# Attention probabilities turned as two halves of 64 queries, in PSUM places of two banks, with a new issue order

## The chip, the core and the metric

The kernel runs on one core of a Trainium2 chip. A core has five engines with queues of their own, which work in order and wait for each other by semaphores: TensorE (PE, matmuls, with weight loads shown apart as PEld), VectorE (DVE), ScalarE (ACT), GpSimd (POOL) and SyncE (SP, which issues DMAs). TensorE's results go to PSUM, eight banks of 512 float32 columns on each of 128 partitions; ScalarE and VectorE read them from there. The metric is the time of the device for one execution, in microseconds (us).

## The reference

Two stages follow each other. The first is attention over 8 batches, 8 heads, 576 positions and 64 channels, with a mask by blocks of 64 positions; the second sends each of the 4608 tokens to one of 8 experts, and at most `capacity` (80) tokens per expert are computed.

```python
scores = scale * np.matmul(q, k.transpose(0, 1, 3, 2))
mask = block_i >= block_j                       # blocks of 64 positions
scores = np.where(mask, scores, -1000000000.0)
scores = scores - np.max(scores, axis=-1, keepdims=True)
attn = np.exp(scores)
attn = attn / (np.sum(attn, axis=-1, keepdims=True) + 1e-09)
out = np.matmul(attn, v)                        # [batch, head, 576, 64]
...
logits = x @ w_gate                             # x: 4608 tokens x 512
expert_idx = np.argmax(logits, axis=1)          # gate_w: the softmax's value there
h = np.maximum(x[tok_idx] @ w1[e], 0.0)         # at most 80 tokens per expert, by gate_w
out[tok_idx] = gate_w[tok_idx, None] * (h @ w2[e])
```

## The kernel before

The attention stage works on 32 pairs of heads, four to a batch. A pair's 576 queries are five row tiles: 0 to 3 have 128 queries each, tile 4 has 64. Row tile u needs the keys up to 128 x (u + 1), so its scores are 128 wide for tile 0 and 512 for tile 3. What a turn does for a pair is cut into pieces (methods of `Pair`):

- `scores(g)` (L428, L435): matmuls of 64 channels each; one head uses the upper and one the lower 64 rows of the array. Group "3" is row tile 3, "20" row tiles 2 and 0, "1" row tile 1. `scores_4` (L444) is row tile 4. They write to one of two PSUM places of two banks (pool `ps_s`, name `sc`).
- `max` (L449), `max_4` (L453): VectorE's maxima, negated. `soft` (L457), `soft_4` (L462): ScalarE's exponentials from PSUM to SBUF (`P`), with the sums of the rows.
- `back(x)` (L490): TensorE turns blocks of 128 queries by 128 keys of the probabilities, so that the keys come to lie on the partitions. One call fills one PSUM bank with four blocks (pool `ps_m`, four banks, name `pm`). "30" and "31" are row tile 3 of either head, "20" the last blocks of tiles 2 and 0, "2" and "1" the others of tiles 2 and 1, "4" row tile 4, "44" its last, narrow block.
- `take("back", x)`: ScalarE (L522) or VectorE (L524) copies such a bank to SBUF (`PT`). The table `TAKE` names the engine.
- `values` (L510): TensorE multiplies the values by `PT`; `take("values", ...)` copies the result to `xT`.
- `prep` (L410, L413): the next pair's q and k are transposed in 32 x 32 blocks by VectorE, and q is scaled by POOL. `flip` (L278): VectorE transposes `xT` for the store.
- `step`: one of the side steps that follow each batch (the logits and the gate), in three places of a turn, over the three turns that begin three turns behind that of the batch's last pair: reciprocal, store and first logits in the first; second logits and two times their transposes and products in the second; gate, spreading and turning in the third.

The order is written out by hand: the list `TURN` is walked once per turn, and each entry (d, piece, ...) issues a piece of the pair d turns ahead or behind. Each engine's queue is the order in which its pieces stand there, and each piece's instructions wait for what they read and for the buffers that they write.

Of the kernel before, what the change touches and what calls it, by code (L numbers as in the profile page):

```python
# [7 lines left out]
F32 = mybir.dt.float32  # L8
# [16 lines left out]
CHUNK = 80  # L25


TAKE = {"back": {"30": "v", "31": "a", "1": "a", "2": "a", "20": "v", "4": "v", "44": "v"}, "values": {0: "a", 1: "a"}}

GROUPS = {"3": ((3, 0),), "20": ((2, 0), (0, 384)), "1": ((1, 0),)}  # L30

# [11 lines left out]
    (0, "max", "20"),
    (0, "soft", 3, 0),
    (0, "soft", 3, 1),
    (-1, "values", 0),
    (0, "soft", 0, 0),
    (0, "soft", 0, 1),
    (-1, "values", 1),
    (0, "step"),  # L50
    (1, "prep", 0),
    (0, "soft", 2, 0),
    (0, "soft", 2, 1),
    (0, "scores", "1"),
    (0, "max", "1"),
    (0, "back", "30"),
    (0, "back", "31"),
    (0, "step"),
    (0, "scores_4"),
    (1, "prep", 1),  # L60
    (-1, "take", "values", 0),
    (0, "take", "back", "31"),
    (0, "take", "back", "30"),
    (0, "soft", 1, 0),
    (0, "soft", 1, 1),
    (0, "max_4"),
    (0, "back", "20"),
    (0, "back", "2"),
    (0, "soft_4"),
    (0, "take", "back", "20"),  # L70
    (0, "take", "back", "2"),
    (-1, "take", "values", 1),
    (0, "step"),
    (0, "back", "1"),
    (0, "take", "back", "1"),
    (-2, "flip"),
)


# [1 line left out]
def tile_attn_moe(ctx, tc, q, k, v, w_gate, w1, w2, capacity, out, xs=None, dbg=None):  # L81
    nc = tc.nc
    B, H, S, D = q.shape
# [40 lines left out]
    for i in range(4):  # L124
        r = slice(32 * i, 32 * i + 32)
# [120 lines left out]
    Pt = []  # L246
    for i in range(2):
        row = [pb.tile([P, 2, P * (t + 1)], F32, name=f"P{i}_{t}") for t in range(NT - 1)]
        Pt.append(row + [pb.tile([P, P * NT], F32, name=f"P{i}_4")])

    VT = [pb.tile([P, 2, D], F32, name=f"vt{i}") for i in range(3)]

# [1 line left out]
    qk = att.enter_context(tc.tile_pool(name="qk", bufs=2, **right))  # L254
    attp = ExitStack()
    ps_s = attp.enter_context(tc.tile_pool(name="ps_s", bufs=2, space=PSUM))
    ps_m = attp.enter_context(tc.tile_pool(name="ps_m", bufs=4, space=PSUM))

    class Batch:
        def __init__(self, b):  # L260
# [27 lines left out]
        def logits(self, half):  # L288

            q0, q1 = ((0, 384), (384, 576))[half]  # L290
            if half == 0:
                self.lgT = sm.tile([P, S], F32, name="lgT", bufs=1)
            lt = ps_m.tile([P, 512], F32, name="pm")
            for pr in range(NP):
                nc.tensor.matmul(lt[32 * pr:32 * pr + 32, 0:q1 - q0], lhsT=wgd[:, pr, :],
                                 rhs=self.xT[:, pr, q0:q1], start=True, stop=True, tile_position=(0, 32 * pr))
            nc.scalar.copy(self.lgT[:, q0:q1], lt[:, 0:q1 - q0])

        def logits2(self, half, ends=(4, NT)):
            la = ps_m.tile([P, 512], F32, name="pm")  # L300
            rs = self.rs
            if half == 0:
                self.lg = sm.tile([P, NT, E], F32, name="lg", bufs=2)
            t0, t1 = (0, *ends)[half:half + 2]
            for t in range(t0, t1):
                n = tokn(t)
                self.turned = nc.tensor.transpose(la[0:n, P * (t - t0):P * (t - t0 + 1)],
                                                  self.lgT[:, tok0(t):tok0(t) + n], ident)
            for u0, u1, n in ((t0, min(t1, NT - 1), P), (NT - 1, t1, BLK)):
                if u0 < u1:  # L310
                    nu = u1 - u0
                    iv = la[0:n, P * (u0 - t0):P * (u1 - t0)].rearrange("p (r c) -> p r c", r=nu * NP)[:, :, 0:2 * E]
# [42 lines left out]

        def turn2(self):
            sp = self.sp
            tp = ps_m.tile([P, 512], F32, name="pm")
            for s_ in range(2):
                for g in range(4):  # L360
                    self.last = nc.tensor.matmul(
                        tp[32 * g:32 * g + 32, 0:8 * NT], lhsT=sameR3[:, 16 - 16 * s_:48 - 16 * s_],
                        rhs=sp[:, 2 * g + s_].rearrange("p t a -> p (t a)"), start=(s_ == 0), stop=(s_ == 1),
                        tile_position=(0, 32 * g))
            nc.vector.tensor_copy(Wt[:, :, :, self.b, :].rearrange("p h t a -> p t a h"),
                                  tp[:, 0:8 * NT].rearrange("p (t a h) -> p t a h", t=NT, h=2))
# [11 lines left out]
    class Pair:  # L378
# [87 lines left out]
        def back(self, x):  # L466


            if x == "30":
                self.PT = big.tile([P, 2, 13, P], F32, name="PT")  # L470
            PT = self.PT
            row = Pt[self.i % 2]
            pt = ps_m.tile([P, 512], F32, name="pm")
            if x in ("30", "31"):
                h = int(x[1])
                blocks = [(3, h, j) for j in range(4)]
                dst = PT[:, h, 3:13:3]
            elif x in ("1", "2"):
                u = int(x)
                blocks = [(u, h, j) for h in range(2) for j in range(2)]  # L480
                dst = PT[:, :, u:u + 4:3]
            elif x == "20":
                blocks = [b for h in range(2) for b in ((0, h, 0), (2, h, 2))]
                dst = PT[:, :, 0:9:8]
            else:
                blocks = [(4, None, j) for j in (range(4) if x == "4" else (4,))]
                dst = PT[:, :, 10:12] if x == "4" else PT[:, 0, 7]
            for n_, (u, h, j) in enumerate(blocks):
                src = row[u] if h is None else row[u][:, h]
                nc.tensor.transpose(pt[:, P * n_:P * (n_ + 1)], src[:, P * j:P * (j + 1)], ident)  # L490
            src = pt[:, 0:P * len(blocks)]
            if len(dst.shape) == 3:
                src = src.rearrange("p (j c) -> p j c", c=P)
            elif len(dst.shape) == 4:
                src = src.rearrange("p (h j c) -> p h j c", h=2, c=P)
            self.out["back", x] = (dst, src)

        def values(self, half):

            av = ps_m.tile([P, 512], F32, name="pm")  # L500
            PT = self.PT
            for j in range(4 + half):
                for h in range(2):
                    lhs = self.vt[:, h, :] if j == 4 else self.vn[:, h, j, :]
                    if half == 0:
                        rhs, c0, end = PT[:, h].rearrange("p b c -> p (b c)")[:, 512 * j:512 + 384 * j], P * j, 512
                    else:
                        b = PT[:, 0, 7] if j == 4 else PT[:, j // 2, 10 + j % 2]
# [128 lines left out]
    for h in (1, 0):  # L637
        pl = pall[h]
# [273 lines left out]
    with tc.For_i(0, again, 1):  # L912
# [24 lines left out]
        step = 1.0  # L937
# [161 lines left out]
```

## Time and profile before

| | |
|---|---|
| Median of 3 runs | 505.89 us (503.77 to 506.04) |
| The profiled execution | 505.98 us, span 504.1 us |
| Busy in the span | PE 465.5 us (92%), DVE 315.6 (63%), ACT 253.8 (50%), POOL 52.8 (10%) |
| First exponential to the last pair's | 11.35 to 350.86 us |
| End of the attention stage | 372.51 us |
| Mean granted clock of TensorE | 0.989 |

Each turn begins, as counted here, with the first exponential of row tile 3 on ScalarE (L457, 128 x 512). A row of a timeline gives the start from the beginning of the span, how long the instruction took, engine, line, operation, what it writes and reads, and how many are merged in the row; in brackets stands the idle time before it, and what ended it. An instruction's length is longer than the distance to the next one where an engine overlaps the end of one with the beginning of the next.

### The profile page before, as it was taken

To read this page: it belongs to the slowest core of one execution; us is meant where nothing else is said; L and a number is where in the kernel's file an instruction comes from. 1 tells how busy PE (TensorE), PEld (TensorE's weight loads), DVE (VectorE), ACT (ScalarE), POOL (GpSimd) and SP (SyncE) were. 2 spreads that over 40 slices of the span, in tenths; PEclk is the share of its full clock that TensorE was granted. 3 is DMA by queue.
4 is the path that set the end of the run, shared out by engine and by line. 5 is a ranking of instruction groups with operands and counts; after the bars stand their busy time and mean duration, and the time that the engine had idled before them with its cause. 6 is when DMAs were issued, how large, how long until landed. Compare 5 with 4: busy or idle time off the path is not lost. (4 is left out here: it accounts for less than half of the span.)

```text
span 504.1 us, 10559 instructions
## 1 busy us (share of the span) xinstructions
PE 465.5 (92%) x3887; PEld 263.1 (52%) x3887; DVE 315.6 (63%) x636; ACT 253.8 (50%) x795; POOL 52.8 (10%) x120
## 2 busy tenths in 40 slices
PE   6999989999999999999999999899877999999993
PEld 3666556556556656655665665565554333333330
DVE  4777787878788788868887886978583311211120
ACT  2776577667556766766665775667520110011000
POOL 1110301010010101001000100100025300100010
PEclk9999999999999999999999999999997999999998
DMA  5776467358647866776688588595484999979110
GB/s 93 135 131 113 75 110 138 61 97 157 106 80 157 178 156 129 148 175 139 147 166 182 129 161 180 117 282 130 167 238 103 349 385 372 411 276 387 56 43 15
DMA packets 232937, 84.11 MB, mean 167 GB/s; under 512 B 196899, under 2 KB 215331, under 8 KB 232880
## 3 DMA queue, kind: packets, MB, share of 16 engines
q1 hardware_dynamic: 231888, 80.93, 65.2%
q0 software_dynamic: 992, 2.43, 1.4%
q8 instruction: 33, 0.54, 0.4%
q14 instruction: 24, 0.20, 0.1%
HBM read 63.21 MB, written 20.59 MB: 166 GB/s over the span
## 5 line engine op out<-in xcount | busy, mean ns | idle before, releaser
L457 ACT ACTIVATE P<-sc,negm 128x512 f32<-128x512 f32 (+3 forms) x256 | 132.7, 528 | 91.9 <-DVE negm L449 85.9
L449 DVE TENSOR_REDUCE negm<-sc 128x2 f32<-128x1024 f32 (+3 forms) x128 | 101.9, 817 | 47.5 <-PE sc L435 47.3
L490 PE MATMUL pm<-ident,P 128*128 128x128 f32 x800 | 112.1, 280 | 10.6 <-DVE prod L313 5.9
L490 PEld LDWEIGHTS pm<-ident,P 128*128 128x128 f32 x800 | 85.3, 140 | 43.7 <-issue 25.7
L428 PE MATMUL sc<-T,T 64*128 64x128 f32 (+3 forms) x512 | 91.5, 473 | 2.1 <-ACT P L457 1.1
L510 PE MATMUL pm<-PT,vn 128*64 128x64 f32 (+4 forms) x1024 | 91.1, 330 | 1.2 <-DVE PT L524 1.1
L524 DVE COPY PT<-pm 128x512 f32<-128x512 f32 (+1 forms) x128 | 70.9, 575 | 11.0 <-PE pm L490 11.0
L510 PEld LDWEIGHTS pm<-PT,vn 128*64 128x64 f32 x1024 | 52.0, 137 | 41.2 <-issue 34.9
L428 PEld LDWEIGHTS sc<-T,T 64*128 64x128 f32 x512 | 42.1, 188 | 31.5 <-issue 8.0
L522 ACT COPY PT<-pm 128x512 f32<-128x512 f32 x96 | 56.4, 589 | 2.1
L859 PE MATMUL ps<-w,xsT 128*64 128x512 f32 (+1 forms) x256 | 53.0, 603 | 0.8 <-ACT xsT L848 0.8
L413 POOL TENSOR_SCALAR T<-T 128x576 f32<-128x576 f32 x32 | 21.5, 671 | 306.8 <-PE pm L510 138.8
L457 ACT ACTIVATION_READ_ACCUMULATOR P<-sc,negm 128x1 f32 x256 | 52.0, 203 | 0.0
L410 DVE STREAM_TRANSPOSE T<-ld 128x576 f32<-128x576 f32 x64 | 48.8, 763 | 3.1 <-DMA ld<-in_q_dram 1.7
L444 PE MATMUL sc<-T,T 64*64 64x288 f32 x256 | 38.0, 415 | 1.3 <-ACT P L457 1.3
L462 ACT ACTIVATE P<-sc,negm 128x576 f32<-128x576 f32 x32 | 23.7, 740 | 24.2 <-DVE negm L453 24.2
L859 PEld LDWEIGHTS ps<-w,xsT 128*64 128x64 f32 (+1 forms) x256 | 15.3, 124 | 28.8 <-issue 27.2
L862 ACT ACTIVATE h<-ps 128x512 f32<-128x512 f32 x12 | 7.2, 598 | 44.5 <-PE ps L859 44.5
L453 DVE TENSOR_REDUCE negm<-sc 128x1 f32<-128x576 f32 x32 | 24.0, 751 | 5.1 <-PE sc L444 5.0
L870 DVE COPY hT<-pm 128x512 f32<-128x512 f32 x12 | 8.0, 686 | 29.8 <-PE pm L869 29.8
L522 ACT COPY xT<-pm 128x512 f32<-128x512 f32 x64 | 26.1, 408 | 0.9 <-PE pm L510 0.9
L278 DVE STREAM_TRANSPOSE Y<-xT 128x576 f32<-128x576 f32 x32 | 24.5, 766 | 0.0
(169 smaller groups left out, 318.7 us busy)
## 6 DMA issues: line engine op xcount, KB each, us to landing
w<-in_moe_w_dram SPq DMA_DIRECT2D x16, 2048.0 KB, 15.1
ld<-in_q_dram SPq DMA_DIRECT2D x128, 72.0 KB, 2.5
ld<-in_k_dram SPq DMA_DIRECT2D x128, 72.0 KB, 2.5
xs<-Y SPq DMA_DIRECT2D x32, 288.0 KB, 4.5
out_dram<-zero SPq DMA_DIRECT2D x18, 512.0 KB, 3.4
vn<-in_v_dram SPq DMA_DIRECT2D x64, 128.0 KB, 2.8
vt<-in_v_dram SPq DMA_DIRECT2D x32, 32.0 KB, 2.7
xs<-rs SPq DMA_DIRECT2D x8, 16.0 KB, 4.4
```

What stands on the lines that cost most here:

```text
L278: nc.vector.transpose(self.Y[:, :, pr], self.xT[:, pr])
L410: nc.vector.transpose(t, self.nat[x].rearrange("p g d -> p (g d)"))
L428: nc.tensor.matmul(s[:, h, c:c + P * (u + 1)], lhsT=self.T[0][r, P * u:P * (u + 1)], rhs=self.T[1][r, 0:P * (u + 1)], start=(x == 0), stop ...
L444: nc.tensor.matmul(s[r, c, 0:288], lhsT=self.T[0][r, 512:S], rhs=self.T[1][r, 288 * c:288 * (c + 1)], start=True, stop=True)
L449: nc.vector.tensor_reduce(self.negm[:, u], self.s[g][:, :, c:c + P * (u + 1)], axis=AX.X, op=ALU.max, negate=True)
L453: nc.vector.tensor_reduce(self.negm[:, 4, 0:1], self.s["4"][:, :, 0:288], axis=AX.XY, op=ALU.max, negate=True)
L457: nc.scalar.activation(Pt[self.i % 2][u][:, h], self.s[g][:, h, c:c + P * (u + 1)], AF.Exp, bias=self.negm[:, u, h:h + 1], scale=1.0, accu ...
L490: nc.tensor.transpose(pt[:, P * n_:P * (n_ + 1)], src[:, P * j:P * (j + 1)], ident)
L510: nc.tensor.matmul(av[h * D:(h + 1) * D, c0:end], lhsT=lhs, rhs=rhs, start=(j == 0), stop=(j == 3 + half))
L522: nc.scalar.copy(*self.out.pop((what, x)))
L524: nc.vector.tensor_copy(*self.out.pop((what, x)))
L859: nc.tensor.matmul(ph[wid * j:wid * (j + 1)], lhsT=xsT[k][:, a, c0:c0 + wid], rhs=w1t[k][:, a, f * 512:(f + 1) * 512], start=(a == 0), sto ...
```

## The change

- `back` now works on halves: the block of 128 queries is read as two halves of 64, each on its own 64 rows of the array, and each half goes to another bank. One call turns eight blocks into one place of two banks. "A" is row tile 3 of both heads, "B" the earlier blocks of row tiles 1 and 2, "C" row tile 4 and the last blocks of tiles 0 and 2. Block "44" is turned without its padding, into a bank that it shares with the values' second part.
- The pool `ps_m` has two places of two banks instead of four of one. The side steps' tiles take a whole place, of which they use one bank.
- Each place is copied out as two takes (A0 and A1, and so on), each over 256 columns of both banks. `TAKE` puts A1, B0, C0, C1 and the values' first part on ScalarE, and A0, B1, 44 and the values' second part on VectorE.
- `TURN` is written in a new order; C, 44 and the values are of the pair before, as 4, 44 and the values were.

```diff
-TAKE = {"back": {"30": "v", "31": "a", "1": "a", "2": "a", "20": "v", "4": "v", "44": "v"}, "values": {0: "a", 1: "a"}}
+TAKE = {"back": {"A0": "v", "A1": "a", "B0": "a", "B1": "v", "C0": "a", "C1": "a", "44": "v"},
+        "values": {0: "a", 1: "v"}}
...
     (0, "scores", "3"),
+    (-1, "back", "C"),
     (0, "scores", "20"),
...
+    PL = [pb.tile([P, P], F32, name=f"pl{i}") for i in range(2)]
...
-    ps_m = attp.enter_context(tc.tile_pool(name="ps_m", bufs=4, space=PSUM))
+    ps_m = attp.enter_context(tc.tile_pool(name="ps_m", bufs=2, space=PSUM))
+
+    def bank():
+        return ps_m.tile([P, 2, 512], F32, name="pm")[:, 0]
...
+            if x == "44":
+                dst = PL[self.i % 2][0:BLK]
+                src = self.mixed()[0:BLK, 1, 0:P]
+                nc.tensor.transpose(src, row[4][:, 512:S], ident)
+                self.out["back", x] = (dst, src)
+                return
...
-            pt = ps_m.tile([P, 512], F32, name="pm")
-            if x in ("30", "31"):
-                h = int(x[1])
-                blocks = [(3, h, j) for j in range(4)]
-                dst = PT[:, h, 3:13:3]
...
+            pt = ps_m.tile([P, 2, 512], F32, name="pm")
+            if x == "A":
+                blocks = [(3, h, j) for h in range(2) for j in range(4)]
+                dst = [PT[:, h, 3:13:3] for h in range(2)]
+            elif x == "B":
+                blocks = [(u, h, j) for u in (1, 2) for h in range(2) for j in range(2)]
+                dst = [PT[:, :, u:u + 4:3] for u in (1, 2)]
             else:
...
+                blocks = [(4, None, j) for j in range(4)] + [b for h in range(2) for b in ((0, h, 0), (2, h, 2))]
+                dst = [PT[:, :, 10:12], PT[:, :, 0:9:8]]
             for n_, (u, h, j) in enumerate(blocks):
                 src = row[u] if h is None else row[u][:, h]
-                nc.tensor.transpose(pt[:, P * n_:P * (n_ + 1)], src[:, P * j:P * (j + 1)], ident)
...
+                for c in range(2):
+                    r = slice(c * BLK, (c + 1) * BLK)
+                    nc.tensor.transpose(pt[:, c, n_ * BLK:(n_ + 1) * BLK], src[r, P * j:P * (j + 1)], ident[r, r])
+            for y in range(2):
+                src = pt[:, :, 256 * y:256 * (y + 1)]
+                self.out["back", f"{x}{y}"] = (
+                    (dst[y].rearrange("p j (r c) -> p r j c", r=2), src.rearrange("p r (j c) -> p r j c", c=BLK))
+                    if x == "A" else (dst[y].rearrange("p h j (r c) -> p r h j c", r=2),
+                                      src.rearrange("p r (h j c) -> p r h j c", h=2, c=BLK)))
...
+    def mixed(self):
+
+            if not hasattr(self, "pv"):
+                self.pv = ps_m.tile([P, 2, 512], F32, name="pm")
+            return self.pv
...
-            av = ps_m.tile([P, 512], F32, name="pm")
+            av = self.mixed()[:, 0] if half == 0 else self.mixed()[:, 1, P:P + BLK]
```

How the queues change around the copies, first VectorE. Before, from the second input transpose of a turn to the copy of "4" (T1 is the transposed k, `sc` scores, `pm` a place of turned blocks or values, PT the turned probabilities, Y the flipped output; a name in brackets is whose semaphore the instruction waits for, 49 being the kernel's number, DMAHW a DMA):

```order
L410 STREAM_TRANSPOSE T1_1432<-ld1_1192 128x576 [waits DMAHW2_49,DMAHW3_49,DMAHW1_49,DMAHW0_49]
L524 COPY PT_1416<-pm_1417 128x4x128 [waits PE_49]
L453 TENSOR_REDUCE negm_1356<-sc_1427 128x1 [waits PE_49]
L524 COPY PT_1416<-pm_1440 128x2x2x128 [waits PE_49]
L278 STREAM_TRANSPOSE Y_671<-xT_670 128x18x32 [waits Activation_49]
L449 TENSOR_REDUCE negm_1475<-sc_1476 128x2 [waits PE_49]
```

And of the changed kernel, from the same transpose to the first max of row tiles 2 and 0:

```order
L413 STREAM_TRANSPOSE T1_1592<-ld1_1336 128x576 [waits DMAHW2_49,DMAHW3_49,DMAHW1_49,DMAHW0_49]
L537 COPY PT_1594<-pm_1595 128x2x4x64 [waits Activation_49]
L456 TENSOR_REDUCE negm_1519<-sc_1616 128x1 [waits PE_49]
L537 COPY PT_1594<-pm_1623 128x2x2x2x64 [waits Activation_49]
L281 STREAM_TRANSPOSE Y_1351<-xT_1350 128x18x32 [waits DVE_49]
L452 TENSOR_REDUCE negm_1657<-sc_1658 128x2 [waits PE_49]
```

The copies of row tile 3's blocks (128x4x128 before, 128x2x4x64 now) and of the next ones (128x2x2x128, now 128x2x2x2x64) stand at the same places, before and behind the max of row tile 4 (L453, now L456). Before they wait for PE; now they wait for Activation: where ScalarE and VectorE read one PSUM tile, the program holds a wait between the two. The max of row tile 3 (L449, now L452) stands behind the flip in both.

ScalarE, before, from the copy of the values to the next pair's first exponential:

```order
L522 COPY xT_1206<-pm_1383 128x512 [waits PE_49]
L522 COPY PT_1416<-pm_1422 128x4x128 [waits PE_49,Activation_49]
L457 ACTIVATE P1_1_131,sums_1208<-sc_1410,negm_1356 128x256 [waits DVE_49]
L457 ACTIVATE P1_1_131,sums_1208<-sc_1410,negm_1356 128x256
L462 ACTIVATE P1_4_134,sums4_1209<-sc_1427,negm_1356 128x576 [waits DVE_49]
L522 COPY PT_1416<-pm_1445 128x2x2x128 [waits PE_49]
L522 COPY xT_1206<-pm_1394 128x64
L522 COPY PT_1416<-pm_1454 128x2x2x128 [waits PE_49]
L457 ACTIVATE P0_3_128,sums_1208<-sc_1476,negm_1475 128x512 [waits DVE_49,Activation_49]
```

And in the changed kernel:

```order
L535 COPY xT_1350<-pm_1552 128x512 [waits DVE_49,PE_49]
L460 ACTIVATE P1_1_131,sums_1352<-sc_1573,negm_1519 128x256 [waits DVE_49,Activation_49]
L460 ACTIVATE P1_1_131,sums_1352<-sc_1573,negm_1519 128x256 [waits Activation_49]
L535 COPY PT_1594<-pm_1595 128x2x4x64 [waits PE_49,Activation_49]
L465 ACTIVATE P1_4_134,sums4_1353<-sc_1616,negm_1519 128x576 [waits DVE_49]
L535 COPY PT_1594<-pm_1623 128x2x2x2x64 [waits PE_49]
L535 COPY PT_1594<-pm_1663 128x2x2x2x64 [waits PE_49]
L535 COPY PT_1594<-pm_1663 128x2x2x2x64
L460 ACTIVATE P0_3_128,sums_1352<-sc_1658,negm_1657 128x512 [waits DVE_49,Activation_49]
```

The copy of row tile 3's blocks moved from before the exponentials of row tile 1 (128x256) to behind them. Behind the exponential of row tile 4 stand three copies of 512 columns, B0 and the two takes of C, before the next pair's first exponential (128x512).

## Rows read from the trace of the kernel before

**Rows 1.** Windows: stretch, length, each engine's busy time, clock, DMA share, GB/s.

```profile
11.35:50.03 38.68, 37.03 (x335) 23.93 (x332) 29.66 (x44) 28.37 (x91) 3.83 (x11) 1.00 0.71 127
50.03:63.10 13.07, 12.57 (x111) 7.57 (x108) 9.15 (x19) 7.26 (x23) 3.81 (x16) 1.00 0.40 73
50.03:72.19 22.16, 20.22 (x185) 12.79 (x183) 16.83 (x30) 14.43 (x46) 4.48 (x17) 1.00 0.45 80
72.19:339.99 267.80, 255.41 (x2409) 159.76 (x2407) 212.65 (x390) 179.43 (x570) 21.26 (x36) 1.00 0.70 147
339.99:350.86 10.87, 10.87 (x102) 6.55 (x100) 8.76 (x16) 7.65 (x25) 0.67 (x1) 1.00 0.68 156
350.86:372.51 21.65, 19.01 (x199) 12.55 (x197) 15.23 (x47) 9.52 (x30) 0.79 (x1) 1.00 0.53 196
151.46:161.40 9.94, 9.94 (x94) 6.42 (x92) 7.98 (x12) 7.27 (x24) 0.67 (x1) 1.00 0.70 154
```

**Rows 2.** Timeline of TensorE, a plain turn: start, length, engine, line, operation.

```profile
157.42 1.53 PE L490 MATMUL pm<-ident,P 128*128 128x128 f32 x12
158.88 1.13 PE L428 MATMUL sc<-T,T 64*128 64x512 f32 x4
```

**Rows 3.** Timeline of ScalarE, the same turn.

```profile
151.46 0.69 ACT L457 ACTIVATE P<-sc,negm 128x512 f32<-128x512 f32 x1 [1.82 <-DVE negm L449]
...
152.14 0.68 ACT L457 ACTIVATE P<-sc,negm 128x512 f32<-128x512 f32 x1
...
153.93 0.37 ACT L457 ACTIVATE P<-sc,negm 128x128 f32<-128x128 f32 x1 [1.03 <-DVE negm L449]
...
154.63 0.58 ACT L457 ACTIVATE P<-sc,negm 128x384 f32<-128x384 f32 x1
...
155.74 0.60 ACT L522 COPY xT<-pm 128x512 f32<-128x512 f32 x1
...
156.95 0.48 ACT L457 ACTIVATE P<-sc,negm 128x256 f32<-128x256 f32 x1
...
157.41 0.48 ACT L457 ACTIVATE P<-sc,negm 128x256 f32<-128x256 f32 x1
...
158.33 0.74 ACT L462 ACTIVATE P<-sc,negm 128x576 f32<-128x576 f32 x1 [0.36 <-DVE negm L453]
...
159.06 0.57 ACT L522 COPY PT<-pm 128x512 f32<-128x512 f32 x1
159.53 0.22 ACT L522 COPY xT<-pm 128x64 f32<-128x64 f32 x1
```

**Rows 4.** Timeline of ScalarE and VectorE where one waits for the other.

```profile
410.92 0.17 ACT L759 COPY gsum<-ps 80x24 f32<-80x24 f32 x1 [1.07 <-PE ps L753]
...
411.12 0.16 DVE L760 TENSOR_TENSOR comb<-gsum 80x8 f32<-80x8 f32 x1 [1.10 <-ACT gsum L759]
```

**Rows 5.** Timeline of VectorE, the same turn as rows 3.

```profile
150.14 1.23 DVE L449 TENSOR_REDUCE negm<-sc 128x2 f32<-128x1024 f32 x1 [1.12 <-PE sc L435]
...
156.00 0.77 DVE L410 STREAM_TRANSPOSE T<-ld 128x576 f32<-128x576 f32 x1
156.69 0.65 DVE L524 COPY PT<-pm 128x512 f32<-128x512 f32 x1
157.54 0.76 DVE L453 TENSOR_REDUCE negm<-sc 128x1 f32<-128x576 f32 x1 [0.20 <-PE sc L444]
158.21 0.68 DVE L524 COPY PT<-pm 128x512 f32<-128x512 f32 x1
158.81 0.77 DVE L278 STREAM_TRANSPOSE Y<-xT 128x576 f32<-128x576 f32 x1
```

**Rows 6.** Groups by form, ScalarE; then VectorE's timeline at the gate.

```profile
L297 ACT COPY lgT<-pm 128x384 f32<-128x384 f32 x8 | 4.0, 498 | 1.5 <-PE pm L295 1.5
...
97.94 0.18 DVE L330 TENSOR_REDUCE mx<-lg 128x5 f32<-128x40 f32 x1
...
99.77 0.78 DVE L410 STREAM_TRANSPOSE T<-ld 128x576 f32<-128x576 f32 x1
```

More of the change, by code (lines that the diff above doesn't have):

```diff
@@ L36 @@
     (0, "scores", "3"),
+    (-1, "back", "C"),
     (0, "scores", "20"),
-    (-1, "back", "4"),
+    (-1, "take", "back", "C1"),
+    (-1, "take", "back", "C0"),
+    (0, "max", "3"),
     (-1, "back", "44"),
-    (0, "max", "3"),
-    (-1, "take", "back", "4"),
+    (-1, "values", 0),
+    (0, "max", "20"),
+    (0, "soft", 3, 1),
+    (1, "prep", 0),
+    (0, "soft", 3, 0),
+    (0, "soft", 2, 1),
+    (0, "soft", 2, 0),
     (-1, "take", "back", "44"),
[L43 to L46, printed above, removed]
+    (0, "step"),
     (0, "soft", 0, 0),
+    (0, "scores", "1"),
+    (-1, "values", 1),
     (0, "soft", 0, 1),
[L49 to L54, printed above, removed]
-    (0, "max", "1"),
-    (0, "back", "30"),
-    (0, "back", "31"),
+    (0, "max", "1"),
+    (-1, "take", "values", 0),
+    (-1, "take", "values", 1),
+    (1, "prep", 1),
+    (0, "back", "A"),
+    (0, "soft", 1, 0),
+    (0, "soft", 1, 1),
+    (0, "take", "back", "A1"),
+    (0, "take", "back", "A0"),
     (0, "step"),
     (0, "scores_4"),
[L60 to L65, printed above, removed]
     (0, "max_4"),
-    (0, "back", "20"),
-    (0, "back", "2"),
     (0, "soft_4"),
-    (0, "take", "back", "20"),
-    (0, "take", "back", "2"),
-    (-1, "take", "values", 1),
     (0, "step"),
-    (0, "back", "1"),
-    (0, "take", "back", "1"),
-    (-2, "flip"),
+    (0, "back", "B"),
+    (0, "take", "back", "B0"),
+    (0, "take", "back", "B1"),
+    (-1, "flip"),
 )
@@ L248, in tile_attn_moe @@
         row = [pb.tile([P, 2, P * (t + 1)], F32, name=f"P{i}_{t}") for t in range(NT - 1)]
-        Pt.append(row + [pb.tile([P, P * NT], F32, name=f"P{i}_4")])
+        Pt.append(row + [pb.tile([P, S], F32, name=f"P{i}_4")])
+    PL = [pb.tile([P, P], F32, name=f"pl{i}") for i in range(2)]
     VT = [pb.tile([P, 2, D], F32, name=f"vt{i}") for i in range(3)]
@@ L292, in logits @@
                 self.lgT = sm.tile([P, S], F32, name="lgT", bufs=1)
-            lt = ps_m.tile([P, 512], F32, name="pm")
+            lt = bank()
             for pr in range(NP):
@@ L299, in logits2 @@
         def logits2(self, half, ends=(4, NT)):
-            la = ps_m.tile([P, 512], F32, name="pm")
+            la = bank()
             rs = self.rs
@@ L357, in turn2 @@
             sp = self.sp
-            tp = ps_m.tile([P, 512], F32, name="pm")
+            tp = bank()
             for s_ in range(2):
@@ L466, in back @@
         def back(self, x):
-            if x == "30":
+            row = Pt[self.i % 2]
+            if x == "44":
[5 more added lines that the diff above has]
+            if x == "A":
                 self.PT = big.tile([P, 2, 13, P], F32, name="PT")
             PT = self.PT
-            row = Pt[self.i % 2]
@@ L473, in back @@
-            pt = ps_m.tile([P, 512], F32, name="pm")
-            if x in ("30", "31"):
-                h = int(x[1])
-                blocks = [(3, h, j) for j in range(4)]
-                dst = PT[:, h, 3:13:3]
[L478 to L484, printed above, removed]
-            else:
-                blocks = [(4, None, j) for j in (range(4) if x == "4" else (4,))]
-                dst = PT[:, :, 10:12] if x == "4" else PT[:, 0, 7]
+            pt = ps_m.tile([P, 2, 512], F32, name="pm")
@@ new lines, in back @@
+            if x == "A":
+                blocks = [(3, h, j) for h in range(2) for j in range(4)]
[3 more added lines that the diff above has]
+                dst = [PT[:, :, u:u + 4:3] for u in (1, 2)]
+            else:
+                blocks = [(4, None, j) for j in range(4)] + [b for h in range(2) for b in ((0, h, 0), (2, h, 2))]
+                dst = [PT[:, :, 10:12], PT[:, :, 0:9:8]]
@@ L488, in back @@
             for n_, (u, h, j) in enumerate(blocks):
                 src = row[u] if h is None else row[u][:, h]
-                nc.tensor.transpose(pt[:, P * n_:P * (n_ + 1)], src[:, P * j:P * (j + 1)], ident)
[L491 to L496, printed above, removed]
+                for c in range(2):
+                    r = slice(c * BLK, (c + 1) * BLK)
+                    nc.tensor.transpose(pt[:, c, n_ * BLK:(n_ + 1) * BLK], src[r, P * j:P * (j + 1)], ident[r, r])
@@ L507, in values @@
                     else:
-                        b = PT[:, 0, 7] if j == 4 else PT[:, j // 2, 10 + j % 2]
+                        b = PL[self.i % 2] if j == 4 else PT[:, j // 2, 10 + j % 2]
                         rhs, c0, end = b[:, h * BLK:(h + 1) * BLK], 0, BLK
@@ L512, in values @@
             self.out["values", half] = ((self.bt.xT[:, self.pr, 0:512], av) if half == 0 else
-                                        (self.bt.xT[:, self.pr, 512:S], av[:, 0:BLK]))
+                                        (self.bt.xT[:, self.pr, 512:S], av))
         def flip(self):
@@ L538, in tile_attn_moe @@
     pairs = [Pair(i) for i in range(n)]
-    for row in Pt:
-        nc.gpsimd.memset(row[4][:, S:], 0.0)
+    for t_ in PL:
+        nc.gpsimd.memset(t_[BLK:P], 0.0)
     for t_ in VT:
@@ L553, in tile_attn_moe @@
     with tc.manual_schedule():
-        warm(WARM[0], ps_m.tile([P, 512], F32, name="pm"))
+        warm(WARM[0], bank())
         for i in range(-2, n + 2):
```

## The prediction

> **What bounds the kernel now.** I read the windows by stretch first, then the timelines of a plain turn, then the order of the changed program. In a plain turn (from the first exponential of one pair to that of the next) TensorE is busy for 9.94 of 9.94 us, VectorE for 7.98 and ScalarE for 7.27 [rows 1]: TensorE sets the pace. Turns that carry a batch's side steps take longer: 24 turns, six batches of four, take 267.80 us, 44.63 a batch, 4.87 more than four plain turns. Of the rest, the first four turns take 38.68 (1.08 less than four plain ones), the turn with the constants and the one behind it 22.16 (13.07 of them the first), the last 10.87, and 21.65 pass from the last pair's first exponential to the end of the attention stage [rows 1]. [...]
>
> **What the change does on TensorE.** Twelve whole transposes take 1.46 us until the scores behind them start, 0.122 each [rows 2]. A pair has 25: 3.05 us. Afterwards 24 blocks are turned as two halves of half the columns. Bounds: if the halves run side by side, a block takes half, 0.061, and the turn's transposes 24 x 0.061 + 0.12 = 1.58; if each half takes its turn for as long as a whole block does now, 48 x 0.122 + 0.12 = 5.98. I take 1.58: scores already run as matmuls on the two row halves, and four of 512 columns take 1.13 together [rows 2], where four times the time of a 128-column transpose, each after the other, would be 4 x 4 x 0.122 = 1.95. So TensorE's work in a turn falls by 1.47, to 8.47 us. If TensorE stayed the limit, 32 turns would give back 47 us.
>
> **Why I don't expect that.** What is late next is a ring of ScalarE and VectorE, closed by the new places. A place holds two takes (A0 and A1, or B0 and B1) over the same two banks; A1 and B0 are on ScalarE, A0 and B1 on VectorE, and in the changed order VectorE's copies A0 and B1 wait for ScalarE, where their counterparts before wait for TensorE alone (the two pieces in the section on the change). Behind A0 in VectorE's queue stand the max of row tile 4, B1, the flip and the max of row tile 3. ScalarE's exponential of row tile 4 waits for that max, B0 and both C copies stand behind it, and then the next pair's exponentials, which wait for the max of row tile 3. TensorE's C transposes, put right behind the scores of row tile 3, wait for that exponential too; TensorE has room for this now. So the two engines take turns around a whole turn, and its length is a sum.
>
> ScalarE, from the first exponential of row tile 3 to the end of A1, start to start [rows 3]: row tile 3, 0.68 + 0.68; row tile 2, two heads, 155.74 - 154.63 = 1.11; row tile 0, 154.63 - 153.93 = 0.70; the copy of the values, 0.47 (159.53 - 159.06, a copy of 512); row tile 1, 2 x 0.46; A1 until it has ended, 0.57. Together 5.13. Then the hand-over to VectorE. The only row of one, after a small copy, gives 411.12 - 411.09 = 0.03 [rows 4]; the hand-over the other way, to the first exponential, took 151.46 - 151.37 = 0.09 [rows 3, 5]. I take 0.05, nearer the row of the same direction. VectorE [rows 5]: A0 0.60 until the max behind it (158.81 - 158.21), that max 0.76, hand-over 0.03 (158.30 to 158.33, [rows 3]). ScalarE: exponential of row tile 4 0.73, B0 0.57, hand-over 0.05. VectorE: B1 0.60, flip 0.69 (the same shape, 156.69 - 156.00), max of row tile 3 1.23, hand-over 0.09. Sum: 5.13 + 0.05 + 0.60 + 0.76 + 0.03 + 0.73 + 0.57 + 0.05 + 0.60 + 0.69 + 1.23 + 0.09 = 10.53 us. That is 0.59 more than the 9.94 of now, though TensorE has 1.47 less to do. The C copies and VectorE's other work lie beside: ScalarE has 1.23 + 0.69 + 0.60 of time while VectorE works for two C copies of 0.57.
>
> **The side steps** cost less than now, since TensorE and much of VectorE have room. On the ring lie: the two copies of logits on ScalarE, about 0.37 and half of that, 0.2 (the first lasts 0.50 of which some 0.13 overlaps the next, [rows 6]); the first of two products on VectorE between A0 and the max, 0.34 (256 elements, half of a copy's 0.60 and a little); and the gate, 99.77 - 97.94 = 1.83 us on VectorE [rows 6], less the room there. That room is ScalarE's 3.64 from the max of row tile 3 to the exponentials of row tile 1, less VectorE's max of row tiles 2 and 0 (1024 columns, 1.2), transpose (0.69), a quarter copy (0.2) and max of row tile 1 (0.65): 0.9. So 0.37 + 0.2 + 0.34 + 0.9 = 1.8 a batch; bounds are 0 and the 4.87 of now. The second product stands where VectorE waits for B0 anyhow.
>
> **The sum**, against the profiled execution's own 505.98 us (span 504.1; the median of the runs, 505.89, is the same to 0.02%):
> - start, six turns: 6 x 10.53, less 1.08 in the first four as now, plus 3.13 for the constants (13.07 - 9.94; the turn behind can't catch up in a ring) = 65.2 against 38.68 + 22.16 = 60.84: +4.4.
> - six batches: 4 x 10.53 + 1.8 = 43.9 against 44.63: -0.7 each, -4.2.
> - last turn: 10.53 + 0.37 = 10.90 against 10.87: 0.
> - from the last first exponential to the end of the stage: +1.1, between 0 and 3. One more round of the ring costs 0.59, and the last logits wait for a place of two banks.
> - later stages shift and don't change: the diff leaves them alone.
> Together +1.3: **507.3 us**. Other edits: the padding tiles are filled by POOL at the start, as many elements as before, beside the first loads; the order of SP's loads is kept, and what SP waits for (the input's transposes on VectorE) keeps its place behind a max; the quarter copy of block 44 loses half its partitions and gains or loses nothing. The steps' single-bank needs now take whole places, so a step's matmuls wait longer; TensorE's 2 us of room a turn hide it, and without that room the waits would cost what steps cost now.
>
> **Rivals.** A, *the ring is open*: the copies of one place don't wait on each other in effect, and TensorE's 8.47 decides: 506 - 47 = 459 us. For it speaks only that TensorE decides now [rows 1]; against it that the wait stands in the order. [...] I give it 0.08 on the order alone.
>
> B, *the copies of halves are longer* (the slower side): A1, A0, B0 and B1 read two banks in runs of 64, and all four stand in the ring. Copies here hardly depend on shape (0.65 and 0.68 for two shapes on VectorE, 0.57 on ScalarE, [rows 3, 5]); if each took 0.1 more, the ring would be 10.93 and the time 507 + 13 = 520. It decides (slower by over 0.5%) from about 0.01 each, 1.1 us over 32 turns. Chance 0.14 for a rise that matters.
>
> C, *the halves gain nothing on TensorE, or its clock falls*: with 48 halves at 0.061 one after the other the transposes take 3.05 as now, and TensorE's 9.94 plus its new waits (for row tile 4's exponential, and for places in the step turns) would cost some 8 us: 515; at the upper bound of 5.98 TensorE's turn is 9.94 + 2.93 = 12.87 and the time about 506 + 94 = 600. Against it: the scores' rows. TensorE will idle some 2 us a turn; in the step turns it already idles (255.41 busy of 267.80) at a clock of 1.00 [rows 1]. [...] Chance 0.08.
>
> **How the numbers follow.** An unchanged kernel is told from a changed one here by about 0.5%, 503.4 to 508.4. The ring gets 0.70: its terms are good to perhaps 0.1 a turn, 3 us, and the steps to 0.3 a batch, 2 us, so 502 to 513; of that 0.46 lies within 0.5%, 0.19 above, 0.05 below. A 0.08, faster; B 0.14 and C 0.08, slower. So faster 0.13, same 0.46, slower 0.41. The range of 8 in 10 is 501 to 518: ring and most of B.
>
> **What would show it.** Plain turns of about 10.5 us with TensorE busy for 8 to 9 of them; VectorE's copy A0 ending its wait on ScalarE's A1, and B1 on B0; a first exponential that waits 1.2 us for the max of row tile 3; pairs of half transposes starting 0.06 apart. Plain turns under 9 us would say that the ring isn't closed; transposes at 0.12 a pair or a clock below 1.00, that C holds; copies over 0.62 us on ScalarE or 0.75 on VectorE, that B does.

## The result, and the profile after

The changed kernel takes 512.22 us (median of 4 runs, 511.69 to 512.50), the kernel before in the same comparison 505.19 (503.77 to 506.04): a ratio of 1.0141, with a 95% interval of 1.0112 to 1.0169. It is slower by 1.4%. The prediction, 507.3 with a range of 501 to 518, held the time; but its likeliest outcome, no difference of 0.5%, did not come about.

The windows of the changed kernel by stretch (columns as in [rows 1]; each stretch begins with a first exponential of row tile 3; the sixth ends with the attention stage, the seventh is a plain turn):

```profile
10.33:53.08 42.75, 36.92 (x430) 21.91 (x432) 29.76 (x46) 29.77 (x92) 3.84 (x11) 0.92 0.67 120
53.08:67.33 14.25, 10.21 (x127) 5.94 (x123) 8.72 (x19) 7.54 (x24) 3.80 (x16) 1.00 0.35 63
67.33:79.29 11.96, 10.32 (x105) 6.18 (x107) 7.62 (x13) 7.64 (x23) 0.67 (x1) 0.71 0.53 95
79.29:345.95 266.66, 233.22 (x2984) 136.33 (x2982) 205.31 (x391) 187.04 (x570) 21.45 (x36) 0.99 0.71 148
345.95:357.10 11.15, 9.90 (x125) 5.54 (x123) 8.60 (x17) 8.01 (x25) 0.67 (x1) 1.00 0.49 119
357.10:379.53 22.43, 17.16 (x215) 11.13 (x212) 13.68 (x46) 9.51 (x29) 0.79 (x1) 1.00 0.52 188
158.34:168.83 10.49, 9.03 (x117) 5.37 (x115) 7.53 (x13) 7.53 (x24) 0.67 (x1) 1.00 0.55 106
```

The plain turn takes 10.49 us where the turn of [rows 1] took 9.94, and TensorE, which was busy for all of it before, now idles for 1.46. TensorE's work fell and the time rose. The timelines of that turn say why. ScalarE first (start, length, operation, idle time before it and what ended it):

```profile
158.34 0.69 ACT L460 ACTIVATE P<-sc,negm 128x512 f32<-128x512 f32 x1 [1.21 <-DVE negm L452]
...
161.13 0.38 ACT L460 ACTIVATE P<-sc,negm 128x128 f32<-128x128 f32 x1
...
161.48 0.61 ACT L535 COPY xT<-pm 128x512 f32<-128x512 f32 x1
...
162.85 0.63 ACT L535 COPY PT<-pm 128x512 f32<-128x512 f32 x1
164.90 0.74 ACT L465 ACTIVATE P<-sc,negm 128x576 f32<-128x576 f32 x1 [1.42 <-DVE negm L456]
...
165.64 0.58 ACT L535 COPY PT<-pm 128x512 f32<-128x512 f32 x1
...
168.83 0.69 ACT L460 ACTIVATE P<-sc,negm 128x512 f32<-128x512 f32 x1 [1.21 <-DVE negm L452]
```

VectorE:

```profile
162.12 0.23 DVE L537 COPY xT<-pm 128x64 f32<-128x64 f32 x1 [0.82 <-ACT xT L535]
...
163.52 0.69 DVE L537 COPY PT<-pm 128x512 f32<-128x512 f32 x1 [0.45 <-ACT PT L535]
164.12 0.75 DVE L456 TENSOR_REDUCE negm<-sc 128x1 f32<-128x576 f32 x1
166.25 0.69 DVE L537 COPY PT<-pm 128x512 f32<-128x512 f32 x1 [1.38 <-ACT PT L535]
166.85 0.77 DVE L281 STREAM_TRANSPOSE Y<-xT 128x576 f32<-128x576 f32 x1
167.55 2.05 DVE L452 TENSOR_REDUCE negm<-sc 128x2 f32<-128x1024 f32 x2
```

TensorE, B and C of the same turn:

```profile
162.99 0.71 PE L497 MATMUL pm<-ident,P 64*128 64x64 f32 x16
163.54 1.08 PE L431 MATMUL sc<-T,T 64*128 64x512 f32 x4
...
165.79 0.71 PE L497 MATMUL pm<-ident,P 64*128 64x64 f32 x16 [1.15 <-ACT P L465]
```

Read the brackets across the engines. ScalarE's A1 (162.85) releases VectorE's A0 (163.52); behind A0 and the max of row tile 4 ScalarE begins that tile's exponential (164.90), then B0 (165.64), which releases VectorE's B1 (166.25); behind B1, the flip and the max of row tile 3 the next pair's first exponential begins (168.83). TensorE waits inside this, for 1.15 us at C, and holds up nothing. Its halves do what was hoped: B's sixteen take 163.54 - 162.99 = 0.55 us until the scores behind them start, where eight whole blocks, at the 0.122 of [rows 2], come to 0.98.

### The profile page after: what moved, and what is told of

Same layout as the page of the kernel before. It is cut to its first block, busy times and chain, and to the rows that moved or that the text cites. A ratio compares the mean times of both kernels' runs of the same rounds, so it can differ in the third digit from the quotient of the medians.

```text
span 509.5 us, 12107 instructions
## 1 busy us (share of the span) xinstructions
PE 438.7 (86%) x4655; PEld 234.5 (46%) x4655; DVE 306.0 (60%) x636; ACT 263.9 (52%) x795; POOL 53.3 (10%) x120
## 5 line engine op out<-in xcount | busy, mean ns | idle before, releaser
L431 PE MATMUL sc<-T,T 64*128 64x128 f32 (+3 forms) x512 | 94.3, 467 | 13.7 <-ACT P L460 12.6
L452 DVE TENSOR_REDUCE negm<-sc 128x2 f32<-128x1024 f32 (+3 forms) x128 | 98.1, 803 | 10.2 <-PE sc L438 10.1
L523 PE MATMUL pm<-PT,vn 128*64 128x64 f32 (+4 forms) x1024 | 98.3, 335 | 0.5 <-DVE mx L333 0.5
L497 PE MATMUL pm<-ident,P 64*128 64x64 f32 x1536 | 70.1, 233 | 28.9 <-DVE PT L537 15.0
L497 PEld LDWEIGHTS pm<-ident,P 64*128 64x128 f32 x1536 | 56.9, 142 | 59.5 <-ACT P L465 22.2
L535 ACT COPY PT<-pm 128x512 f32<-128x512 f32 x128 | 72.5, 593 | 13.3 <-PE pm L497 13.3
L537 DVE COPY PT<-pm 128x512 f32<-128x512 f32 x64 | 44.3, 692 | 58.3 <-ACT PT L535 58.2
L460 ACT ACTIVATION_READ_ACCUMULATOR P<-sc,negm 128x1 f32 x256 | 54.4, 212 | 0.0
L447 PE MATMUL sc<-T,T 64*64 64x288 f32 x256 | 40.0, 433 | 1.1 <-ACT P L460 0.6
L456 DVE TENSOR_REDUCE negm<-sc 128x1 f32<-128x576 f32 x32 | 24.0, 748 | 0.6 <-PE sc L447 0.6
L889 PE MATMUL ps<-w,hT 128*64 128x512 f32 (+1 forms) x128 | 23.3, 595 | 0.0
```

What stands on the lines that cost most here:

```text
L431: nc.tensor.matmul(s[:, h, c:c + P * (u + 1)], lhsT=self.T[0][r, P * u:P * (u + 1)], rhs=self.T[1][r, 0:P * (u + 1)], start=(x == 0), stop ...
L447: nc.tensor.matmul(s[r, c, 0:288], lhsT=self.T[0][r, 512:S], rhs=self.T[1][r, 288 * c:288 * (c + 1)], start=True, stop=True)
L452: nc.vector.tensor_reduce(self.negm[:, u], self.s[g][:, :, c:c + P * (u + 1)], axis=AX.X, op=ALU.max, negate=True)
L456: nc.vector.tensor_reduce(self.negm[:, 4, 0:1], self.s["4"][:, :, 0:288], axis=AX.XY, op=ALU.max, negate=True)
L460: nc.scalar.activation(Pt[self.i % 2][u][:, h], self.s[g][:, h, c:c + P * (u + 1)], AF.Exp, bias=self.negm[:, u, h:h + 1], scale=1.0, accu ...
L497: nc.tensor.transpose(pt[:, c, n_ * BLK:(n_ + 1) * BLK], src[r, P * j:P * (j + 1)], ident[r, r])
```

## The experiments

Each time is the median of its kernel, the ratio that to the kernel before in the same comparison, with its 95% interval. Edits are to the changed kernel.

### Both copies of a place on one engine

```diff
-TAKE = {"back": {"A0": "v", "A1": "a", "B0": "a", "B1": "v", ...
+TAKE = {"back": {"A0": "a", "A1": "a", "B0": "v", "B1": "v", ...
```

> Edit: both copies of a place on one engine (A0 and A1 on ScalarE, B0 and B1 on VectorE), so each engine has as many copies as in the changed kernel and neither waits for the other's copy of the same place. Ring theory (ScalarE and VectorE take turns, because the two copies of a place wait on each other): the alternation opens, plain turns fall from 10.49 us to what TensorE needs, 8.5 to 9.0, and the time to 460 to 475. Rival (TensorE's waits for only two places, and its clock, set the pace): the number of places is the same, so plain turns stay at 10.4 to 10.6 and the time at 508 to 516.

Measured: 479.23 us, ratio 0.9487 (0.9466 to 0.9507). Two letters in a table are worth 33 us (512.22 - 479.23). A plain turn, as a window:

```profile
184.52:193.33 8.81, 8.67 (x117) 5.25 (x115) 7.56 (x13) 7.58 (x23) 0.67 (x1) 1.00 0.71 156
```

ScalarE and VectorE are as busy as in the changed kernel (7.58 and 7.56, then 7.53 and 7.53), in a turn that is 1.68 us shorter. So neither was short of time: what was lost is order. The time lies 4 us above the range of the expectation, for not all turns gain as the plain ones do: those with side steps take 10.08, 11.13 and 10.30, and the first six together 61.08, no less than the 60.84 of the kernel before [rows 1]. The rival, two places as the limit, falls.

### Whole transposes again, with the ring closed and open

```diff
-                for c in range(2):
-                    r = slice(c * BLK, (c + 1) * BLK)
-                    nc.tensor.transpose(pt[:, c, n_ * BLK:(n_ + 1) * BLK], src[r, P * j:P * (j + 1)], ident[r, r])
+                nc.tensor.transpose(pt[:, n_ % 2, P * (n_ // 2):P * (n_ // 2 + 1)], src[:, P * j:P * (j + 1)], ident)
```

(The copies' patterns follow; each still reads 256 columns of both banks. The kernel with the ring open has the table of the experiment above as well.)

> Edit: the changed kernel with whole 128 x 128 transposes again, into the same places, with the same copies, engines and order; only TensorE's work grows, by some 1.47 us a turn. Ring theory: TensorE's 9.03 busy of 10.49 becomes about 10.5, just hidden; plain turns 10.5 to 10.9, time 512 to 525. Rival (TensorE sets the pace): every turn grows by 1.47, time about 555 to 560. If halves gain nothing on TensorE: time 512 and TensorE's busy time in a plain turn unchanged at 9.0.

> Both edits: copies of a place on one engine, and whole transposes. Ring theory: with the ring open TensorE is the limit, and whole transposes cost their full 1.47 us a turn: 30 to 47 us more than the kernel with the copies on one engine and halves, so 495 to 515, near the kernel before. Rival (halves gain nothing): the same time as that kernel.

Measured: ring closed 520.02 us (ratio 1.0290, 1.0260 to 1.0319), ring open 509.81 (1.0109, 1.0082 to 1.0136). Windows of a plain turn, first two of the kernel with the ring closed (an early one, and one behind a gate):

```profile
42.45:52.94 10.49, 10.39 (x93) 6.38 (x91) 7.63 (x13) 7.53 (x23) 0.77 (x2) 1.00 0.51 94
...
297.54:308.61 11.07, 10.98 (x95) 6.65 (x97) 7.65 (x13) 7.64 (x24) 0.67 (x1) 1.00 0.56 113
```

and of the one with the ring open:

```profile
154.89:165.22 10.33, 10.33 (x94) 6.39 (x92) 7.75 (x12) 7.76 (x25) 0.67 (x1) 1.00 0.63 139
```

The early turn shows that TensorE doesn't set the pace of the changed kernel: it has 1.36 us more work (10.39 against 9.03), and the turn is 10.49 as in the changed kernel. With the ring open the same work costs 10.33 - 8.81 = 1.52 a turn, near the 1.47 of the prediction. Halves are thus worth 30.6 us where TensorE is the limit (509.81 - 479.23), and 7.8 in the kernel as it was changed (520.02 - 512.22), the latter in turns where TensorE's work reaches past the ring's length, like the one behind a gate (10.98 busy of 11.07).

### One of the two waits alone

```diff
-TAKE = {"back": {"A0": "v", ...      first kernel
+TAKE = {"back": {"A0": "a", ...
-..."B0": "a", ...                    second kernel
+..."B0": "v", ...
```

> Edit: the changed kernel with copy A0 on ScalarE as well as A1; B0 and B1 stay on both engines. Ring theory, by the rows of the changed kernel's plain turn: VectorE's A0 and the max of row tile 4 no longer stand between A1 and the exponential of row tile 4. From the first exponential 4.51 us to A1, two copies 0.48 + 0.58, then 0.74 + 0.61 + 0.60 + 0.70 + 1.28 as before: 9.50 in place of 10.49; 9.7 if the max of row tile 4 comes late. Time 480 to 492. If either wait alone keeps the ring as long as it is: 10.4 to 10.5, 508 to 514.

> Edit: the changed kernel with copy B0 on VectorE as well as B1; A0 and A1 stay on both engines. Ring theory: the exponential of row tile 4 and B0's wait leave the ring, VectorE goes from the max of row tile 4, which begins 5.78 us after the first exponential, straight on: 5.78 + 0.67 + 0.60 + 0.60 + 0.70 + 1.28 = 9.63 in place of 10.49. Time 483 to 495. If either wait alone keeps the ring as long as it is: 10.4 to 10.5, 508 to 514.

Measured: A alone 486.41 us (ratio 0.9634, 0.9609 to 0.9659), plain turns 9.49, as the sum said. B alone missed: 507.55 (1.0030, 1.0006 to 1.0054), and plain turns of 9.95 in place of 9.63. ScalarE, VectorE and TensorE in such a turn of the second kernel:

```profile
44.86 0.59 ACT L535 COPY xT<-pm 128x512 f32<-128x512 f32 x1 [0.22 <-PE pm L523]
...
48.27 0.74 ACT L465 ACTIVATE P<-sc,negm 128x576 f32<-128x576 f32 x1 [1.42 <-DVE negm L456]
```

```profile
46.88 0.69 DVE L537 COPY PT<-pm 128x512 f32<-128x512 f32 x1 [0.44 <-ACT PT L535]
```

```profile
49.15 0.71 PE L497 MATMUL pm<-ident,P 64*128 64x64 f32 x16 [1.00 <-ACT P L465]
```

A second ring, 0.54 us shorter than the first, stands behind it. From the exponential of row tile 4 (48.27) it is 0.88 to TensorE's C, from there 5.66 through the scores, the values and ScalarE's copy of them (44.86 + 9.95 = 54.81), and 3.41 on, through row tile 1, A1, VectorE's A0 that waits for it (46.88) and the max of row tile 4, to the next exponential of row tile 4: 9.95. The expectation counted two engines where three were tied, which makes some 10 us (32 x 0.32). Another 7 us are the clock: in the turns with the gate TensorE waits 1.69 us for a place, and in five of the six its granted clock falls, as in this window of such a turn and the next, 11.74 and 10.41 where the first such pair, at a clock of 1.00, took 10.95 and 9.71 (the five pairs lose 1.4 to 1.5 each):

```profile
192.49 1.12 PE L497 MATMUL pm<-ident,P 64*128 64x64 f32 x16 [1.69 <-DVE PT L537]
```

```profile
185.47:197.21 11.74, 9.52 (x127) 6.01 (x123) 9.84 (x23) 7.27 (x23) 1.47 (x2) 0.85 0.70 172
197.21:207.62 10.41, 9.41 (x118) 5.58 (x120) 8.34 (x14) 7.25 (x23) 0.67 (x1) 1.00 0.50 93
```

### A piece of the ring moved out of it

```diff
     (0, "max", "20"),
+    (-2, "flip"),
...
-    (-1, "flip"),
```

> Edit: the changed kernel with VectorE's flip (0.69 us) taken out of the stretch between copy B1 and the max of row tile 3 and put, for the pair before, behind the max of row tiles 2 and 0, where VectorE otherwise waits. Ring theory: plain turns fall by that 0.69 to 9.80, also the first six and the turn of the second step; the turns with the reciprocal and the gate, whose slack is used up, do not gain. Some 18 turns by 0.69: 12 us less, 497 to 503. Rival (TensorE or its places set the pace): 510 to 514.

Measured: 508.69 us, ratio 1.0087 (1.0059 to 1.0115); plain turns 10.18. In the expected direction, but above the expected range: plain turns gain 0.31 and not 0.69. The turn's first exponential waits less (0.54 for 1.21), and the copy of the values now waits for TensorE:

```profile
44.40 0.39 ACT L460 ACTIVATE P<-sc,negm 128x128 f32<-128x128 f32 x1
...
45.12 0.59 ACT L535 COPY xT<-pm 128x512 f32<-128x512 f32 x1 [0.24 <-PE pm L523]
```

From the exponential to that copy it is now 0.72 us; in the changed kernel it is 161.48 - 161.13 = 0.35. That gives back 0.37 of the 0.69: the same second ring, longer by 0.23 than with B alone (10.18 against 9.95). The moved flip holds up VectorE's copy of block 44, and TensorE now waits for that copy before the values' second part:

```profile
54.45 0.69 PE L523 MATMUL pm<-PT,vn 128*64 128x64 f32 x16 [0.15 <-DVE pl L537]
```

In three of the six turns with the gate the granted clock also falls here, to a mean of 0.86. They take 12.34, 12.42 and 12.44 for 11.58, and the turns behind them 10.61 to 10.62 for 10.18, 3.8 us together.

### One tile for each half

The blocks' halves c go to tiles of one bank each (`pt[c]` in place of `pt[:, c]`), four such places in all; a copy reads one of them, and `PT` has 16 blocks in place of 13, so that C's targets fit one pattern. The two parts of the values, which shared a place of two banks, have a bank each. Engines and order stay.

```diff
-    ps_m = attp.enter_context(tc.tile_pool(name="ps_m", bufs=2, space=PSUM))
+    ps_m = attp.enter_context(tc.tile_pool(name="ps_m", bufs=4, space=PSUM))
...
-            pt = ps_m.tile([P, 2, 512], F32, name="pm")
+            pt = [bank(), bank()]
...
-                src = pt[:, :, 256 * y:256 * (y + 1)]
...
+                r = slice(y * BLK, (y + 1) * BLK)
+                self.out["back", f"{x}{y}"] = (dst[..., r], pt[y].rearrange(k, h=2, j=4 if x == "A" else 2, c=BLK))
```

> Edit: the changed kernel with four places of one bank instead of two of two banks; halves, engines of the copies and order stay. Each half goes to a tile of its own, a copy reads one tile (all eight blocks of one half of the queries), so A0 and A1, and B0 and B1, share none and the program holds no wait between them. Ring theory (the wait between the copies, not which engine makes them, closes the alternation): opens it as the kernel with both copies on one engine did, plain turns 8.5 to 8.9, time 465 to 480. Rival (that kernel gained by its other allotment of copies to the engines): plain turns near 10.5, time 505 to 515.

Measured: 465.56 us, ratio 0.9209 (0.9177 to 0.9242). A plain turn, and then ScalarE's B0 and VectorE's B1 in it:

```profile
175.94:184.78 8.84, 8.84 (x116) 5.45 (x115) 7.47 (x13) 7.61 (x24) 0.67 (x1) 1.00 0.76 163
```

```profile
183.05 1.73 ACT L527 COPY PT<-pm 128x512 f32<-128x512 f32 x3
```

```profile
182.21 0.68 DVE L529 COPY PT<-pm 128x512 f32<-128x512 f32 x1
```

B1 now begins 0.84 us before B0, where it waited for B0's end; TensorE is busy for the whole turn and is the limit again. So it was the wait, not which engine makes the copy. The rival falls. With both copies on one engine the plain turn was as short (8.81); the further 13.7 us lie in the other turns, those with side steps (9.66, 10.77 and 9.41 for 10.08, 11.13 and 10.30) and the first six (58.25 for 61.08). A side step's tile takes one of four places here and one of two there; no run separates that from the rest.

The values' two copies show that the wait goes by the tile and not by the bank. Both write `xT` in either kernel. In the changed kernel the two parts lie in different banks of one tile, ScalarE copies the first and VectorE the second, and VectorE waited 0.82 us for ScalarE's end (162.12 above). With a tile for each part the second copy can begin in the middle of the first:

```profile
62.34 0.61 ACT L527 COPY xT<-pm 128x512 f32<-128x512 f32 x1
```

```profile
62.44 0.22 DVE L529 COPY xT<-pm 128x64 f32<-128x64 f32 x1 [0.28 <-PE pm L515]
```

### Constants a turn earlier, alone and on one-bank places

```diff
+            if i == 4:
+                constants1()
             if i == 5:
```

`constants1` holds the iotas for `iota_c` and `iota_p` and the copy to `cf`, three POOL instructions taken out of `constants2`.

> Edit: the changed kernel with three small POOL operations of the constants (a copy, two iotas) issued a turn earlier, so that VectorE no longer waits 2.14 and 0.36 us for POOL in the constants turn. In the changed kernel that turn is followed by 8 us at half TensorE clock (67 to 75 us), behind 3.7 us in which TensorE did nothing. If the clock fell because of that idle stretch: the turn falls from 14.25 to about 11.75, the next from 11.96 to 10.5, 4 us together, time about 508. If the clock falls at that place anyhow: 2.5 us, time about 509.7, and the next turn stays at 11.96.

> Both edits, one-bank places and the three constants a turn earlier. If they add: 3 to 4 us less than one-bank places alone, 462 to 476. If the constants turn then has other waits behind it: the same as one-bank places alone.

Measured: alone 508.66 us (ratio 1.0050, 1.0030 to 1.0070), with one-bank places 461.80 (0.9122, 0.9089 to 0.9154), at the lower edge of what was expected. Windows of the constants turn and the next, for the edit alone:

```profile
53.70:65.34 11.64, 10.18 (x127) 5.95 (x123) 8.58 (x19) 7.54 (x24) 2.88 (x11) 1.00 0.43 77
65.34:75.83 10.49, 7.88 (x107) 4.79 (x107) 7.53 (x13) 7.53 (x23) 1.33 (x5) 1.00 0.50 89
```

Against 14.25 and 11.96 these are 2.61 and 1.47 less, and the clock stays at 1.00. In the changed kernel it was this, in windows of 2 us:

```profile
64.00:66.00 2.00, 0.76 (x10) 0.37 (x6) 0.62 (x4) 0.00 (x0) 1.65 (x7) 1.00 0.00 0
66.00:68.00 2.00, 0.00 (x0) 0.00 (x0) 2.00 (x3) 0.67 (x2) 0.00 (x0) 0.91 0.00 0
68.00:70.00 2.00, 1.17 (x6) 0.66 (x6) 1.28 (x4) 2.00 (x9) 0.67 (x1) 0.50 0.00 0
```

TensorE does nothing in the second (it stood still for 4.07 us in all, not the 3.7 of the expectation) and comes back at a granted clock of 0.50, which it keeps in the next two windows, to 74.00. The gains of the two edits add up: 461.80 is 3.8 less than one-bank places alone, 44 less than the kernel before, and the fastest kernel here.

### VectorE's gate away from POOL

```diff
-    (1, "prep", 0),
...
     (0, "step"),
+    (1, "prep", 0),
     (0, "soft", 0, 0),
```

> Edit: the changed kernel with the transpose of the next pair's q put behind the side step in VectorE's queue, so that POOL's scaling of q begins after the gate's subtraction. In six of eight gates that subtraction took 0.60 us, POOL's scaling beside it, and 0.20 in the two where POOL did nothing. If POOL's work beside it is the cause: 0.20 in all, and the turn with the gate falls from 11.58 to about 11.2, time 508 to 511 unless another step turn loses it. If not: 0.60 stays, 511 to 513.

Measured, one run: 512.04 us. The subtraction takes 0.20 in all eight, as the cause required, but the gate's turn is not shorter: 11.68 for 11.58, where 11.2 was expected. The copy of block 44, which the transpose used to precede, now comes early enough to wait for TensorE, and the transpose stands between the gate and the max of row tile 1: 4.10 us from the first exponential to that max (145.51 to 149.61), where it was 3.96.

## Why the prediction was right, and where its sum was off

**The ring: right, nearly to the digit.** Up to A0's start 5.13 + 0.05 = 5.18 us were predicted, 163.52 - 158.34 = 5.18 measured; A0 0.60 and 0.60; the max with its hand-over 0.79 and 0.78; the exponential 0.73 and 0.74; B0 with its hand-over 0.62 and 0.61; B1 0.60 and 0.60; the flip 0.69 and 0.70; the max of row tile 3 with its hand-over 1.32 and 1.28. Together 10.53 and 10.49. The experiments show the mechanism: the waits gone, 8.84; the first alone gone, 9.49; TensorE's load raised, 10.49. With the second alone gone it is 9.95, where a ring that the prediction didn't have stands behind it.

**TensorE: right in what halves are worth, too low in the turn.** Pairs of halves start some 0.065 us apart (B's sixteen, 0.22 each, last 0.71 together), and against whole blocks in the same order they save 1.36 to 1.52 us a turn, as predicted (1.47). But the turn's work is not the 8.47 of the prediction: it is 9.03 in the changed kernel, and 8.84 with one-bank places, where TensorE is the limit. What else the change does costs TensorE some 0.4, 10.33 with whole blocks and the ring open for 9.94 before, and the prediction took that as nothing. Of the 47 us that 32 turns "would give back" if TensorE stayed the limit, 40.6 come with one-bank places (506.16 - 465.56).

**Rivals.** A (the ring is open) is out: the waits are there and cost what the ring says; it took other tiles, or other engines for the copies, to open it. B (longer copies) is out: ScalarE's copies in the ring take 0.58 to 0.63 where 0.57 to 0.60 stood, VectorE's 0.69 where 0.65 and 0.68 stood [rows 3, 5], and from the start of A0, as of B1, to that of the next instruction it is 0.60 as before. Of C the first half (no gain on TensorE) is out, and the second, a falling clock, came in part (0.71 in the turn behind the constants, 0.85 in one gate's turn).

**The sum's terms** (predicted +1.3; the profiled executions, 511.69 and 505.98, are 5.7 apart):

- Start, six turns: 68.96 us for 65.2, that is +8.1 and not +4.4. This step failed most: "6 x 10.53, less 1.08 in the first four as now, plus 3.13 for the constants" took for granted that TensorE comes back from each idle stretch at full clock, as the step turns of [rows 1] do. In the constants turn it had been busy for 12.57 of 13.07; now it is for 10.21 of 14.25, and the turn behind, at a granted clock of 0.71, is 11.96, 1.43 over the prediction. Moving the constants takes that away. The first two turns (10.33 and 11.43, the first at 0.67) are 1.8 over it as well, the constants turn itself 0.6.
- Batches: a steady batch, without a fallen clock, takes 11.15 + 11.06 + 11.58 + 10.49 = 44.28 for 43.9, the six 266.66 for 263.6, so -1.1 and not -4.2. The steps cost 2.3, not 1.8: the reciprocal was left out (its three kinds of instruction delay the max of row tile 1, and with it ScalarE by 0.3), and the gate's nine instructions take 2.09 where 1.83 stood, the subtraction of the last section among them. One batch lost 1.0 more, in a gate's turn with a clock of 0.85 (11.76) and the turn behind it (11.28).
- Last turn +0.3 for 0; to the end of the stage 22.43 for 21.65, +0.8 for +1.1.
- Not in the sum: the first exponential came 1.0 earlier (10.33 for 11.35), and the later stages, which the diff leaves alone, took 1.6 less. Over the kernels here the first lies between 10.3 and 11.5 and the later stages between 128.6 and 131.6 us, in no order that follows the edits; I read both as no effect of the change, and their cause stays open.

So to the +1.3 come 3.7 at the start and 3.1 in the batches, and 2.6 go for what was not in the sum: 5.5 of the 5.7 us. That the last item makes up for part of the others is luck; without it the time would be about 514, still in the range.

**What stays open.** That TensorE's chain through C and the values is the second ring is read from the rows of two kernels; no run opens it alone. When the clock falls in a gate's turn is open too: the changed kernel has the same wait of TensorE there in each of six batches, 1.69 us, and the clock fell in the first of them only.

## What to carry to other kernels

Before taking work off the engine that is busy all the time, add up the longest path that the other engines' waits for each other close over one round: if that sum is near the round's length, the work comes off without a gain. A tile that two engines read was a wait in this program, even where they read different banks of it (0.82 us at the copies of the values); give each reader a tile and a bank of its own, as the one-bank places did here (465.56 us for 512.22), and look at the order of the copies, not at how busy the engines are. And work out what the bounding engine does while it idles: a TensorE that waits may come back at half its clock (0.50 behind 4.07 us of idling in the changed kernel), so that a stall elsewhere is paid for again in the next turn, as here with 2.6 us for the constants and 1.5 behind them.

## What the hardware showed beside this

The gate's subtraction on VectorE in the changed kernel, 40 elements a partition with both inputs in SBUF, takes 0.60 us where POOL scales q beside it:

```profile
148.83 0.60 DVE L335 TENSOR_TENSOR dl<-lg,mx 128x40 f32<-128x40 f32 x1
```

```profile
148.71 0.67 POOL L416 TENSOR_SCALAR T<-T 128x576 f32<-128x576 f32 x1 [10.24 <-DVE pl L537]
```

Both end at about 149.4. In the two gates without POOL's work, and in all eight once the transpose had moved, it took 0.20 us. Beside POOL's scaling the subtraction is thus 0.40 us longer; whether it waits in that time or runs more slowly, no row shows.

ScalarE and VectorE read different banks of PSUM at once without a loss here. The copies A1 and A0 in the kernel with one-bank places, which lie over each other, last 0.58 and 0.65 us, as copies of [rows 3, 5] did with 0.57 and 0.65:

```profile
180.73 0.58 ACT L527 COPY PT<-pm 128x512 f32<-128x512 f32 x1
```

```profile
180.65 0.65 DVE L529 COPY PT<-pm 128x512 f32<-128x512 f32 x1
```

No run here shows two engines reading one bank at once.
